# First loads of a two-layer attention and MLP kernel: bias rows and the second token tile on ScalarE's queue, key weights second on SyncE's queue, and a planner that counts some loads differently

## The chip, the cores and the metric

The kernel runs on one core of one Trainium2 chip. The metric is device time in microseconds (us). Times in a profile count from its first instruction. Engines are named as in the profile: PE is TensorE (matmuls), PEld its weight loads, DVE VectorE, ACT ScalarE, POOL GpSimd, SP SyncE, which issues nearly all DMAs. ACT can issue DMAs too; both feed the same DMA engines.

## What is computed

Two layers, each of a sliding-window attention and an MLP, both on a layer norm of the running x and both added to it. Tokens S = 2048, width D = 1024, hidden width F = 3584, 32 heads of 32; each token attends to itself and to 7 earlier tokens at a distance of 2, 4, ... 14.

```python
def _A_ref(x, wqkv, wo):
    H = 32; Dh = D // H
    W, dil = 8, 2
    qkv = (x @ wqkv).reshape(B, S, 3, H, Dh).transpose(2, 0, 3, 1, 4)
    ...
    logits = jnp.einsum("bhsd,bhswd->bhsw", q, kg) * scale
    attn = _softmax(jnp.where(mask, logits, -1e9), axis=-1)
    o = jnp.einsum("bhsw,bhswd->bhsd", attn, vg)
    return o.transpose(0, 2, 1, 3).reshape(B, S, D) @ wo

def _B_ref(x, w1, b1, w2, b2):
    r = jnp.maximum(x @ w1 + b1, 0)
    return (r * r) @ w2 + b2

x = x + _A_ref(_layernorm(x), A_wqkv, A_wo)
x = x + _B_ref(_layernorm(x), B_w1, B_b1, B_w2, B_b2)
# and the same two lines again with the same weights
```

## The kernel before, in words

**Units.** The work is cut into eight units, four blocks of 512 tokens in each of two layers. A unit's block is four token tiles of 128 rows. Even and odd tokens are held apart, so that a window is eight neighbours. A unit u goes through these stages, and TensorE interleaves the stages of neighbouring units:

- SA: load the four tiles, normalize, transpose into xnT (hidden width on the partitions).
- Projections: for keys (wk), queries (wq) and values (wv), eight chunks of 128 columns each (L481), and ACT copies each PSUM result to SBUF (L490: kT, qT, vT).
- S2: DVE multiplies shifted windows (product, L508), sums and softmax, and the values (L621 to L626). In unit 0 TensorE does the sums over a head's 32 columns (reduce, L520, into lg).
- SW: output projection (L671), add the residual (L674), normalize again.
- SF_up and SF_down: the MLP (L696, L721), with relu and square on ACT (L699, L701).

**What sets the order.** Each operation is entered into a planner (class _Plan) with an engine, an estimated duration, what it reads and writes, and for a DMA its bytes. The planner simulates the engines and issues operations by due time; each engine then runs its instructions in the order that came out. Operations marked main (nearly all of TensorE's) keep their written order. The simulation counts a DMA at DMA_RATE plus DMA_LAT, adds DMA_RAMP's second number of us once when the bytes moved pass its first number, and counts a further `lag` us between an operation's end and what depends on it. These numbers move instructions; they are not instructions. `issue_behind(a, b, ...)` makes the planner issue the named operations in that order.

**Memory.** All matmul results and PE transposes share six PSUM banks (tag "mm"). Weights share five SBUF buffers of 1 MB (tag "w"). The tiles of unit 1 and later, and the residual tiles, share two buffers (tag "xt").

**The opening** (first_projections, L752). TensorE first multiplies zeros (spin, L749: 11 matmuls of 512 columns, 6 of 128, and 2 more between the two transposes). Unit 0's tiles are normalized by DVE statistics (L370, L372), two small ACT steps (L373 lnv, L374 rstd), one DVE step (L388) and eight PE transposes (L403); DVE and ACT copy them out (L406, L407, L409). DVE's order there is written by hand: norm0 waits for tile 1's aggregate. Then come, in this order on TensorE: the key projections of the first 256 tokens in five chunks at once, step by step with the four pieces of the key weights as they land, then chunks 5 to 7; tile 2's transposes; the query projections of the first 256 tokens in the same way with the four query pieces, tile 3's transposes in their middle, then chunks 5 to 7; the second 256 tokens; the values.

**The loads of the opening.** SP issues (L418, L352) the tiles 0 and 1 of x, 256 KB each, four key pieces of 512 KB, tiles 2 and 3, four query pieces, then unit 1's first tile, the first half of the value weights, b1 (7 KB, L331), b2 (broadcast to 256 KB, L332), unit 1's next tile, and so on. ACT issues one small load (touch, L440) whose data nobody reads. SP waits, from the eighth load on, for an earlier landing before it issues the next, since eight completion semaphores are used in turn. b1 is transposed by one PE instruction (L334) and copied (L335) late in the opening.

**Unit 1's tiles** (and all later ones) are normalized on ACT: a sum (L380), the mean (L381), a sum of squares (L382), lnv (L384), rstd (L385), nmr (L386) and the normalized tile (L394); SP then issues a transposing DMA (L411).

Of the kernel before, what the change touches and what calls it, by code (L numbers as in the profile page):

```python
# [7 lines left out]
BF = mybir.dt.bfloat16  # L8
# [53 lines left out]
class _Plan:  # L62
# [5 lines left out]
    DMA_RATE = 390e3  # L68
    DMA_LAT = 2.2
    DMA_TR = 2.9  # L70
    DMA_RAMP = (600e3, 1.8)
    SMALL_FIRST = 1000.0

    @classmethod
# [90 lines left out]
    def schedule(self):  # L165
# [19 lines left out]
        while events:  # L185
# [19 lines left out]
            for e in self.ENGINES:  # L205
# [3 lines left out]
                while waiting[e]:  # L209
# [22 lines left out]
                    if op.dma:  # L232
                        if moved < self.DMA_RAMP[0] <= moved + abs(op.dma):
                            dma_free += self.DMA_RAMP[1]
                        moved += abs(op.dma)
# [24 lines left out]
class _Kernel:  # L260
# [61 lines left out]

    def load_biases(self):
        nc, add, KF, D = self.nc, self.plan.add, self.KF, self.D
        rows = self.plan.buf(self.small, [32, 128], BF, "b1rows")
        pt = self.plan.buf(self.ps, [128, 32], BF, "b1ps", "mm", 6)

        def zero():
            nc.vector.memset(rows.t[:], 0.0)
        add("DVE", 0.1, zero, w=[rows])  # L330
        add("SP", 0.5, lambda: nc.sync.dma_start(rows.t[:KF, :], self.b1.rearrange("(c p) -> c p", p=128)), w=[rows], dma=4e3)  # L331
        add("SP", 0.7, lambda: nc.sync.dma_start(self.b2b[:], self.b2.rearrange("(o d) -> o d", o=1).to_broadcast((128, D))), dma=262e3)  # L332
        self.plan.issue_behind(self.opened, self.plan.ops[-2], self.plan.ops[-1])
        add("PE", 0.1, lambda: nc.tensor.transpose(pt.t[:], rows.t[:], self.ident[0:32, 0:32]), r=[rows], w=[pt], main=True)  # L334
        add("DVE", 0.1, lambda: nc.vector.tensor_copy(self.b1T[:], pt.t[:, 0:KF]), r=[pt])  # L335


# [72 lines left out]
        else:  # L410
            add("SP", 1.25, lambda: nc.sync.dma_start_transpose(dst(), xn.t[:]), r=[xn], w=[lo, hi], dma=-690e3, lag=0.4)  # L411

    def load_x(self, layer, t, tag="xt", n=2):
        nc, D = self.nc, self.D
        b = self.plan.buf(self.sb, [128, D], F32, "xt", tag, n)
        if layer == 0:
            b.view = lambda: b.t[:].bitcast(BF)[:, 0:D]
            self.plan.add("SP", 0.5, lambda: nc.sync.dma_start(b.view(), self.par_tile(self.x_par, t)), w=[(b, 0), (b, 1)], dma=262e3)  # L418
        else:
            b.view = lambda: b.t[:]  # L420
            self.plan.add("SP", 0.55, lambda: nc.sync.dma_start(b.view(), self.xs[layer - 1][t * 128:(t + 1) * 128, :]),
                          w=[(b, 0), (b, 1)], dma=524e3, after=self.xs_parts[layer - 1, t])
        return b


    def SA(self, u):
        layer, b = divmod(u, self.NB)
        xnT = self.plan.buf(self.sb, [128, self.KD, BLK], BF, "xnT", "xnT", 2)
        self.state[u]["xnT_A"] = xnT
        first = u == 0  # L430
        if first:
            ops = self.plan.ops
            xts = [self.load_x(layer, tl, "xm", 4) for tl in range(4)]
            x0, x1, x2, x3 = ops[-4:]
            self.state[u]["wk"] = self.w_qkv(self.D, pieces=2)
            k = ops[-4:]
            self.state[u]["wq"] = self.w_qkv(0, pieces=2)
            q = ops[-4:]
            touch = self.plan.buf(self.small, [128, 32], BF, "touch")
            self.plan.add("ACT", 0.4, lambda: self.nc.scalar.dma_start(  # L440
                touch.t[:], self.wqkv.rearrange("(p e) n -> p e n", p=128)[:, 0, self.D:self.D + 32]), w=[touch], dma=8e3)
            self.plan.issue_behind(x0, x1, *k, x2, x3, *q)
            self.opened = q[-1]
        for tl in range(4):
            xt = xts[tl] if first else self.load_x(layer, b * 4 + tl)
            if u == 1:
                self.plan.issue_behind(self.opened, self.plan.ops[-1])
            norm = lambda tl=tl, xt=xt: self.layer_norm(xt, xnT, tl, dve_stats=first, pe_transpose=first)
            if first:
                yield norm  # L450
            else:
                norm()
# [406 lines left out]
```

## Time and profile before

| | |
|---|---|
| runs shown | 1236.03 us median of three, 1235.96 to 1236.37 |
| profiled execution | 1237.49 us, its span 1235.8 us |
| clock granted to TensorE | 1.000 |
| DMA | 255.16 MB, mean 206 GB/s |
| L696, L721, L481 on PE | 388.1, 388.3, 336.3 us busy |

The page gives the busy time and share of each engine and the chain of work that ended last: followed back from the last instruction, at each step to what released it, or to the instruction ahead of it on its engine. A row of the chain in order of time reads: start, length, engine and tile, line, number of instructions. "issue" is time in which an engine waited for nothing that the profile shows, and SPq is SP's queue. A row of a timeline reads: start, length from the first start to the last end, engine, line, operation, output from input with shapes and types, how many follow each other, and in square brackets the idle time of the engine ahead of it with what ended that. Ends of matmuls are modelled: they are pipelined, so their lengths overlap and their starts tell the pace. A row of a table by windows reads: the window, its length, busy time and number of instructions for PE, PEld, DVE, ACT and POOL, the granted clock, the mean share of the 16 DMA engines, and GB/s.

### The profile page before, as it was taken

Reading aid. Unit: us, or ns where it says so; the run is one execution under the profiler, and the core shown is the slowest. Engines: PE = TensorE matmul, PEld = TensorE weight load, DVE = VectorE, ACT = ScalarE, POOL = GpSimd, SP = SyncE. Lnnn points to the kernel's source line nnn. Section 1 sums busy time; section 2 is a strip of 40 time slices with the busy share of each in tenths; the row PEclk is TensorE's granted clock in tenths of the full one; section 3 lists DMA queues with packets and bytes.
Section 4 is the critical chain, followed back from the end, with each engine's and each line's share of the span. In section 5 each row is a group of like instructions: output and inputs, shape, how many; then the busy total and the mean of one; then the engine's idle time right before and its main releaser. Section 6 shows DMA issues by size and latency. Waiting matters only on the chain.

```text
span 1235.8 us, 15619 instructions
## 1 busy us (share of the span) xinstructions
PE 1228.7 (99%) x5914; PEld 638.4 (52%) x5914; DVE 825.3 (67%) x1233; ACT 565.4 (46%) x1031; POOL 180.2 (15%) x200
## 2 busy tenths in 40 slices
PE   8999999999999999999999999999999999999999
PEld 7765444554455544555445554455544564444444
DVE  5899885698806987079870899609885198972001
ACT  5627920488104881158801588016870146612720
POOL 1352000050500200005050020000505011000000
PEclk9999999999999999999999999999999999999999
DMA  6858767677567985588755996549965496567441
GB/s 231 254 189 223 220 215 229 187 231 222 170 213 186 264 249 167 191 222 277 218 187 171 247 282 214 175 152 283 261 206 174 165 255 199 165 191 235 151 136 55
DMA packets 258421, 255.16 MB, mean 206 GB/s; under 512 B 70602, under 2 KB 221354, under 8 KB 258346
## 3 DMA queue, kind: packets, MB, share of 16 engines
q1 hardware_dynamic: 258202, 254.16, 68.1%
q8 instruction: 46, 0.75, 0.3%
q14 instruction: 29, 0.24, 0.1%
q10 hardware_dynamic: 144, 0.01, 0.0%
HBM read 209.99 MB, written 12.58 MB: 180 GB/s over the span
## 4 chain that ended last, share of the span: by engine, by line
PE 98%; DMA 1%; ACT 0%; SPq 0%; issue 0%; DVE 0%
PE ph L696 31%; PE py L721 31%; PE pq L481 26%; PE py L671 9%; DMA xt<-in_A_x_dram 1%; DMA wt<-in_A_wqkv_dram 1%; PE lg L520 0%; ACT xn L382 0%; ACT xn L380 0%; SPq L352 0%; SPq L418 0%; DVE xo L731 0%; ACT qT L490 0%; ACT nmean L381 0%; PE b1ps L334 0%
## 5 line engine op out<-in xcount | busy, mean ns | idle before, releaser
L721 PE MATMUL py<-wt,r2t 128*128 128x512 bf16 (+1 forms) x1820 | 388.3, 376 | 0.0
L696 PE MATMUL ph<-xnT,wt 128*128 128x512 bf16 x1792 | 388.1, 379 | 0.1
L481 PE MATMUL pq<-xnT,wt 128*128 128x512 bf16 (+2 forms) x1674 | 336.3, 362 | 1.5 <-ACT qT L490 1.4
L721 PEld LDWEIGHTS <-r2t 128*128 128x128 bf16 x1820 | 178.1, 98 | 209.0
L481 PEld LDWEIGHTS <-wt 128*128 128x128 bf16 x1674 | 229.9, 144 | 106.3 <-issue 2.8
L696 PEld LDWEIGHTS <-wt 128*128 128x128 bf16 x1792 | 175.2, 98 | 211.5 <-issue 0.6
L490 ACT CAST kT<-pq 128x512 bf16<-128x512 f32 (+1 forms) x72 | 38.6, 543 | 353.5 <-PE pq L481 353.5
L699 ACT ACTIVATE r<-ph,b1T 128x512 bf16<-128x512 f32 x224 | 152.4, 682 | 70.8 <-PE ph L696 70.7
L508 DVE TENSOR_TENSOR P<-qT,kT 128x2048 bf16<-128x2048 bf16 x128 | 154.0, 1235 | 10.6 <-ACT qT L490 5.0
L621 DVE TENSOR_TENSOR pr<-pb,vT 128x2048 bf16<-128x2048 bf16 x128 | 153.4, 1234 | 7.3 <-DMA pb<-p 7.2
L701 ACT ACTIVATE r2t<-r 128x512 bf16<-128x512 bf16 x224 | 139.1, 628 | 5.3
L731 DVE TENSOR_TENSOR xo<-py,xm 128x512 bf16<-128x512 f32 (+1 forms) x33 | 22.3, 675 | 159.2 <-PE py L721 155.8
L624 DVE TENSOR_TENSOR pr<-pr 128x1024 bf16<-128x1024 bf16 (+1 forms) x256 | 126.8, 552 | 0.0
L525 DVE TENSOR_TENSOR P<-P 128x2048 bf16<-128x2048 bf16 x98 | 118.9, 1221 | 1.2
L671 PE MATMUL py<-wt,oT 128*128 128x512 bf16 x512 | 111.8, 379 | 0.0
L674 DVE TENSOR_TENSOR xm<-py,xt 128x512 f32<-128x512 f32 x64 | 43.1, 684 | 94.9 <-PE py L671 94.0
L497 POOL COPY vhalo<-vT 128x7 bf16<-128x7 bf16 x64 | 59.3, 939 | 228.8 <-ACT vT L490 228.7
L497 POOL COPY khalo<-kT 128x7 bf16<-128x7 bf16 x64 | 20.0, 315 | 483.2 <-ACT kT L490 483.0
L471 POOL COPY vT<-vhalo 128x7 bf16<-128x7 bf16 x32 | 68.2, 2183 | 123.6 <-DVE pr L621 123.5
L671 PEld LDWEIGHTS <-oT 128*128 128x128 bf16 x512 | 50.1, 98 | 60.1
L735 DVE TENSOR_TENSOR xm<-py,xm 128x512 f32<-128x512 f32 x32 | 22.0, 690 | 84.1 <-PE py L721 84.1
L373 ACT ACTIVATE lnv<-mv,eps 128x1 f32<-128x1 f32 x36 | 10.5, 291 | 92.6 <-DVE mv L372 92.5
(61 smaller groups left out, 545.7 us busy)
## 6 DMA issues: line engine op xcount, KB each, us to landing
wt<-in_B_w_dram SPq DMA_DIRECT2D x56, 1024.0 KB, 7.0
wt<-in_B_w_dram SPq DMA_DIRECT2D x64, 896.0 KB, 4.8
wt<-in_A_wqkv_dram SPq DMA_DIRECT2D x44, 1024.0 KB, 6.2
wt<-in_A_wo_dram SPq DMA_DIRECT2D x16, 1024.0 KB, 5.8
xt<-xs SPq DMA_DIRECT2D x32, 512.0 KB, 3.6
xt<-in_A_x_dram SPq DMA_DIRECT2D x32, 256.0 KB, 3.3
pb<-p SPq DMA_DIRECT2D x64, 128.0 KB, 5.1
xs<-xm SPq DMA_DIRECT2D x32, 256.0 KB, 3.4
```

Source lines behind the costliest of these rows:

```text
L471: add("POOL", 0.2, lambda: nc.gpsimd.tensor_copy(dst.t[:, 0:off], prev.t[:, c0, :]), r=[(prev, c0)], w=[(dst, 0)])
L481: nc.tensor.matmul(pq.t[:, a - t0:b - t0], w[:, kd % 4, c0:D:8], xnT.t[:, kd, a:b], start=first and kd == k0, stop=last and kd == k1 - 1, ...
L497: add("POOL", 0.2, lambda: nc.gpsimd.tensor_copy(halo.t[:, c0, :], dst.t[:, BLK:BLK + HALO]), r=[(dst, 2)], w=[(halo, c0)])
L508: st["dve"].append(add("DVE", 1.14, lambda: nc.vector.tensor_tensor(P.t[:], q.t[:, hb * HB:(hb + 1) * HB].rearrange("q (g t) -> q g t", g= ...
L525: self.state[u]["dve"].append(self.plan.add("DVE", 1.14, lambda: self.nc.vector.tensor_tensor(a.t[:], a.t[:], b.t[:], ALU.add), r=[b], w=[a]))
L621: dve.append(add("DVE", 1.14, lambda v=v, pr=pr: nc.vector.tensor_tensor(pr.t[:], pb.t[:], _win_ap(v.t, HALO + hb * HB, HB, groups=G), ALU ...
L624: dve.append(add("DVE", d, lambda pr=pr, k=k: nc.vector.tensor_tensor(pr.t[:, :, 0:k, :], pr.t[:, :, 0:k, :], pr.t[:, :, k:2 * k, :], ALU. ...
L671: nc.tensor.matmul(py.t[:], st["o", c].t[:, tl * 128:(tl + 1) * 128], st["wo"][db].t[:, c, :], start=(c == 0), stop=(c == self.NCH - 1))
L696: nc.tensor.matmul(ph.t[:], wt.t[:, kd, cc * 128:(cc + 1) * 128], xnT.t[:, kd, :], start=(kd == 0), stop=(kd == self.KD - 1))
L699: add("ACT", 0.58, lambda ph=ph, r=r, f=f: nc.scalar.activation(out=r.t[:], in_=ph.t[:], func=ACTF.Relu, bias=self.b1T[:, f:f + 1], scale= ...
L701: add("ACT", 0.54, lambda r=r, r2t=r2t: nc.scalar.activation(out=r2t.t[:], in_=r.t[:], func=ACTF.Square), r=[r], w=[r2t])
L721: nc.tensor.matmul(py.t[:], r2[kf].t[:, tl * 128:(tl + 1) * 128], wt.t[:, kf - k0, c0:c1], start=(kf == 0), stop=(kf == KF - 1))
```

## The change

- Unit 0's second tile (tl == 1) is loaded from ACT's queue, behind the rows of b1, which are now loaded there first. The small load "touch" is gone.
- SP's order begins with tile 0 and the four key pieces, then tiles 2 and 3 and the query pieces. b1 is no more among SP's loads.
- The tile of b1's rows has 28 rows rather than 32, so the DVE memset of it is gone, and the PE transpose has 28 columns.
- The planner counts a ramp of 0.4 us rather than 1.8 at 600 KB, and unit 1's tiles 2.0 us later (lag).

```diff
-    DMA_RAMP = (600e3, 1.8)
+    DMA_RAMP = (600e3, 0.4)
...
     def load_biases(self):
-        rows = self.plan.buf(self.small, [32, 128], BF, "b1rows")
+        rows = self.b1rows
         pt = self.plan.buf(self.ps, [128, 32], BF, "b1ps", "mm", 6)
-
-        def zero():
-            nc.vector.memset(rows.t[:], 0.0)
-        add("DVE", 0.1, zero, w=[rows])
-        add("SP", 0.5, lambda: nc.sync.dma_start(rows.t[:KF, :], self.b1.rearrange("(c p) -> c p", p=128)), w=[rows], dma=4e3)
         add("SP", 0.7, lambda: nc.sync.dma_start(self.b2b[:], self.b2.rearrange("(o d) -> o d", o=1).to_broadcast((128, D))), dma=262e3)
-        self.plan.issue_behind(self.opened, self.plan.ops[-2], self.plan.ops[-1])
-        add("PE", 0.1, lambda: nc.tensor.transpose(pt.t[:], rows.t[:], self.ident[0:32, 0:32]), r=[rows], w=[pt], main=True)
+        self.plan.issue_behind(self.opened, self.plan.ops[-1])
+        add("PE", 0.1, lambda: nc.tensor.transpose(pt.t[:, 0:KF], rows.t[:], self.ident[0:KF, 0:KF]), r=[rows], w=[pt], main=True)
...
-    def load_x(self, layer, t, tag="xt", n=2):
+    def load_x(self, layer, t, tag="xt", n=2, eng="SP", lag=0.0):
...
-            self.plan.add("SP", 0.5, lambda: nc.sync.dma_start(b.view(), self.par_tile(self.x_par, t)), w=[(b, 0), (b, 1)], dma=262e3)
+            self.plan.add(eng, 0.47, lambda: (nc.sync if eng == "SP" else nc.scalar).dma_start(b.view(), self.par_tile(self.x_par, t)),
+                          w=[(b, 0), (b, 1)], dma=262e3, lag=lag)
...
-            xts = [self.load_x(layer, tl, "xm", 4) for tl in range(4)]
+            self.b1rows = rows = self.plan.buf(self.small, [self.KF, 128], BF, "b1rows")
+            b1 = self.plan.add("ACT", 0.47, lambda: self.nc.scalar.dma_start(rows.t[:], self.b1.rearrange("(c p) -> c p", p=128)), w=[rows], dma=7e3)
+            xts = [self.load_x(layer, tl, "xm", 4, "ACT" if tl == 1 else "SP") for tl in range(4)]
             x0, x1, x2, x3 = ops[-4:]
+            self.plan.issue_behind(b1, x1)
...
-            touch = self.plan.buf(self.small, [128, 32], BF, "touch")
-            self.plan.add("ACT", 0.4, lambda: self.nc.scalar.dma_start(
-                touch.t[:], self.wqkv.rearrange("(p e) n -> p e n", p=128)[:, 0, self.D:self.D + 32]), w=[touch], dma=8e3)
-            self.plan.issue_behind(x0, x1, *k, x2, x3, *q)
-            self.opened = q[-1]
+            self.plan.issue_behind(x0, *k, x2, x3, *ops[-4:])
+            self.opened = ops[-1]
...
-            xt = xts[tl] if first else self.load_x(layer, b * 4 + tl)
+            xt = xts[tl] if first else self.load_x(layer, b * 4 + tl, lag=2.0 if u == 1 else 0.0)
```

What the planner makes of it, by the built programs (each row is an order on one engine; "xn0 of unit 1" is its first tile):

```
ACT before: ... kT x6, lnv, rstd, kT, lnv, rstd, kT, L380 xn0 of unit 1, L381, L382, qT x6, L380, ...
ACT after:  ... kT x2, lnv, kT, rstd, kT x2, lnv, kT, rstd, kT x2, L380 xn0 of unit 1, qT x5, L381, L382, qT x2, L380, ...
PE:   one group of 8 matmuls (L481) stands behind the first lg reduction instead of ahead of it, and is made up for ahead of the third
DVE:  the second softmax's reciprocal (L600) stands ahead of the first product of the values instead of behind four chunks
SP:   unit 0's two first residual tiles are issued in turn with unit 1's third and fourth transposing DMA instead of behind both
```

Behind unit 1's stages the orders are the same again. Lines of the kernel below the change shift by five.

More of the change, by code (lines that the diff above doesn't have):

```diff
@@ L437, in SA @@
             self.state[u]["wq"] = self.w_qkv(0, pieces=2)
-            q = ops[-4:]
-            touch = self.plan.buf(self.small, [128, 32], BF, "touch")
-            self.plan.add("ACT", 0.4, lambda: self.nc.scalar.dma_start(
-                touch.t[:], self.wqkv.rearrange("(p e) n -> p e n", p=128)[:, 0, self.D:self.D + 32]), w=[touch], dma=8e3)
-            self.plan.issue_behind(x0, x1, *k, x2, x3, *q)
-            self.opened = q[-1]
+            self.plan.issue_behind(x0, *k, x2, x3, *ops[-4:])
+            self.opened = ops[-1]
         for tl in range(4):
-            xt = xts[tl] if first else self.load_x(layer, b * 4 + tl)
+            xt = xts[tl] if first else self.load_x(layer, b * 4 + tl, lag=2.0 if u == 1 else 0.0)
             if u == 1:
```

## The prediction

> **What bounds the kernel now.** I read the page first, then the chain of work that ended last, then the timelines of TensorE and ScalarE around the only long hole that the chain shows, then the DMA rates of the opening.
>
> ```profile
> span 1235.8 us, 15619 instructions
> PE 1228.7 (99%) x5914; PEld 638.4 (52%) x5914; DVE 825.3 (67%) x1233; ACT 565.4 (46%) x1031; POOL 180.2 (15%) x200
> PE 98%; DMA 1%; ACT 0%; SPq 0%; issue 0%; DVE 0%
> ```
>
> TensorE is busy for 99% of the span and is 98% of the chain. So a change of loads can only win what TensorE loses in the opening, and can lose anywhere that it makes TensorE wait. The chain in order of time shows where the opening ends:
>
> ```profile
> 2.72 8.03 DMA wt<-in_A_wqkv_dram
> 10.75 0.02 issue
> 10.77 10.18 DMA xt<-in_A_x_dram
> 20.95 0.02 issue
> 20.97 1.16 ACT xn L380 x2
> 22.13 0.02 issue
> 22.16 0.21 ACT nmean L381
> 22.37 0.02 issue
> 22.39 1.24 ACT xn L382 x2
> 23.63 0.27 ACT qT L490
> 23.90 0.04 issue
> 23.94 6.27 PE pq L481 x56
> ```
>
> From 23.94 us to the end the chain is TensorE alone, but for 0.13 us at 113.5 and the last store. Before that it runs through something that TensorE does not need yet: the first token tile of unit 1 (L418, issued at 10.77, landed at 20.95) and its statistics on ScalarE (L380 to L382). The two timelines say why this stops TensorE:
>
> ```profile
> 19.16 3.35 PE L481 MATMUL pq<-xnT,wt 128*128 128x256 bf16 x28
> 23.94 0.27 PE L481 MATMUL pq<-xnT,wt 128*128 128x256 bf16 x1 [1.44 <-ACT qT L490]
> ```
>
> ```profile
> 20.97 1.06 ACT L380 ACTIVATE xn<-xt 128x1024 bf16<-128x1024 bf16 x1 [4.47 <-DMA xt<-in_A_x_dram]
> ...
> 23.54 1.72 ACT L490 CAST qT<-pq 128x256 bf16<-128x256 f32 x6
> ```
>
> ScalarE runs in order. L380 stands ahead of the evictions of the query projections and waits 4.47 us for its tile; all six "mm" banks are full, and TensorE waits for the first eviction. The idle time is 1.44 us by the modelled end of a matmul (22.51); matmuls of this width start 0.11 apart and last 0.27, so some 1.6 us are lost (22.34 to 23.94). Call the restart R; it is 23.94. What follows R is 1211.9 us of dense work.
>
> **The change, part by part.** R is the later of two times: when TensorE gets there by itself, and when ScalarE has freed a bank.
>
> *ScalarE's order* (lag of 2.0 and the ramp figure; both are the planner's counts and cost no instruction). In the built order L380 of unit 1's first tile is now followed by five qT evictions, and L381 and L382 come after these; the load's place on SP's queue stays. The first eviction then starts 1.09 after the tile lands (20.95 to 22.04: the 1.06 of L380 and its 0.19 read, overlapped) instead of 23.54. From that eviction's start to R it takes 0.40 as now (23.54 to 23.94). With the tile landing as now, R would be 22.44: 1.50 saved. The removed 1.5 us of L381 and L382 run after the five evictions, under 5.4 us of matmuls.
>
> *The load stream.* SP's second load leaves its queue, so the four key pieces are issued one slot earlier: 0.47 (1.27 for 1.74). ScalarE's queue issues the bias rows and the second tile, 0.40 each as the touch load took; ScalarE idles 3.49 before its first instruction at 5.58, which hides it. The touch and the late bias load (0.95 on SP at 12.86) go; nobody waited for either, and SP then waits for earlier landings anyway. What more the stream gains hangs on its slow start:
>
> ```profile
> 2.00:4.00 2.00, 2.00 (x6) 0.76 (x5) 0.44 (x1) 0.08 (x1) 0.40 (x2) 1.00 0.83 269
> 4.00:6.00 2.00, 2.00 (x13) 0.92 (x10) 2.00 (x5) 0.39 (x2) 0.00 (x0) 1.00 0.64 200
> 6.00:8.00 2.00, 1.32 (x21) 1.01 (x18) 1.67 (x5) 0.68 (x4) 0.00 (x0) 1.00 0.95 359
> 8.00:12.00 4.00, 3.95 (x43) 3.43 (x40) 0.42 (x1) 1.10 (x2) 0.00 (x0) 1.00 1.05 400
> 12.00:16.00 4.00, 3.96 (x36) 3.70 (x34) 3.17 (x7) 2.97 (x11) 0.00 (x0) 1.00 1.06 391
> ```
>
> The last column is GB/s. Against 395 the first three stretches are short by 2x126, 2x195 and 2x36, that is 714 KB or 1.8 us. Nothing here proves what a second queue or the missing touch does to that, so the stream's gain lies between 0 and 0.47 + 1.8 = 2.3 us (below 0 only through the second tile, a rival). I take 1.0: the slot and about a third of the shortfall, nearer to the end that needs nothing unseen. Behind 8 us the stream runs at its full rate, so a gain at the start is carried to every landing after it, unit 1's tile too: 19.95, and the bank is free at 21.44.
>
> [...]
>
> *TensorE by itself.* Its first projection starts at 8.18, when piece one lands (1.74 + 6.4 = 8.1), but also when the transposes of tiles 0 and 1 are over (7.54 + 0.62 = 8.16). Those hang on DVE's chain from the tiles: statistics at 3.56, and the third of them needs tile 1 by about 4.8 (it lands at 1.27 + 3.3 = 4.6). So earlier key weights alone start nothing earlier. From 8.18 to 22.34 TensorE then loses, by distance of starts, 0.20 and 0.20 for key pieces three and four (the weight loader shows 0.27 and 0.28), 0.13 for tile 2 at 16.06 and 0.07 for the last query piece: 0.6. A stream earlier by 1.0 removes these, so TensorE arrives at 21.7. Were tiles 0 and 1 normalized 0.1 earlier, without the touch's 8 KB beside them, 21.6. The bank is free at 21.44, so R = 21.7: **2.2 us less**. A stream gaining more than 1.0 adds nothing, since TensorE is the limit from there.
>
> *Statistics of tiles 2 and 3 on ScalarE.* Their lnv now stands behind two key evictions instead of six. Behind it wait six evictions, and TensorE for their banks. Tile 2's mv came 2.0 after it landed (14.8; landed about 12.8), so 13.8 now; the third eviction is done 0.3 later, at 14.2, and its bank is wanted by tile 2's transposes at about 15.4. Cover 1.2; without the stream's gain about 0.2. Nothing.
>
> *Order behind R.* One group of eight matmuls moves behind the first lg reduction, which now comes 6 x 0.895 = 5.4 after R. DVE's four products take 4 x 1.17 = 4.7 from R, so 0.6 of cover is left of 1.5. DVE's second reciprocal (0.55) moves into its 0.88 wait for pb: slightly better. POOL's one swap and the missing memset (0.11) are nothing. Unit 1's third and fourth tile are normalized later: adding the reordered ScalarE rows behind R, the last L394 ends near R+25.6, where it was 45.18 = R+21.2. Their DMA transposes now stand behind two residual loads. In before SP's issue of them was held to 53.26 by a full DMA queue, and unit 1's projections start at about 58; I estimate 1 to 2 us of cover left. Nothing, with a rival.
>
> *Sum.* Of the profiled execution (1237.49, span 1235.8) this leaves a span of 1233.6 and 1235.3. The median of the runs shown is 1236.03, 1.46 below that execution; the same 2.2 off it gives **1233.8**.
>
> **The rivals.**
>
> 1. *The stream hardly moves.* For it: the 16 engines are full from 8 us on, and no row shows the shortfall to be the queue's. At a gain of 0.47, key piece four lands at 11.64 and tile 2 is ready 0.3 late, TensorE arrives at 22.0 and the bank is free at 21.97: 1.9 saved, 1234.1. At 0 it is 1.5 saved, 1234.5. [...] Chance 0.22.
>
> 2. *Tiles 0 and 1 come earlier too.* The touch is gone and tile 1 has a queue of its own. DVE's chain can move until its transposes meet the end of the warm-up matmuls (6.14, where 6.81 stands now): 0.6. With the stream 1.5 earlier R is 21.0: 2.9 saved, 1233.1. Against it: tile 1 now shares the engines with the key weights. Chance 0.18.
>
> 3. *Slower: the second tile starves.* On ScalarE's queue it runs beside key weights that were behind it. DVE's third statistic holds up tile 0's aggregate as well, so every us of landing after 4.8 delays the first projection. R = 21.66 + d reaches 23.94 at d = 2.3, so it decides from a landing at 7.1. Behind all four pieces (2.1 MB at 395 GB/s, 5.3 us) it lands at 9.9: d = 5.1, R = 26.8, 1238.9. Against it: the touch, issued from that queue at 0.83, landed 2.9 later, beside tiles 0 and 1. Chance 0.06.
>
> 4. *Unit 1's late transposes.* If the queue delays them beyond their cover, TensorE stops at unit 1's key projections, near 56 us; 1 to 3 us, so 1234.8 to 1236.8. Chance 0.10.
>
> **How the numbers follow.** The forecast has 0.44, with a range of its own from 1233.4 to 1234.2. The range of 1233.0 to 1235.2 leaves out rival 3, most of rival 4 and the low half of rival 2, under 2 in 10. 0.2% is 2.5 us, about what a measurement of this kernel can tell from no change, so "faster" begins below 1233.56: rival 2 and some 4 in 10 of the forecast, 0.36. "Slower" is rival 3 and a trace of rival 4, 0.07. The rest, 0.57, is within.
>
> **What would show it.** Right: L380 waits less than 4.47 and five qT follow it; TensorE's longest idle time behind 8 us is under 0.3; R is 21.4 to 22.0; the key pieces land about 1.0 earlier than 8.1, 9.4, 10.7 and 12.1; 4 to 6 us runs well above 200 GB/s; no idle time near 56 us. Wrong: tile 1 lands after 4.8 and the first projection starts later than 8.2; a wait for lg's products near R+5.4; or a saving that differs from the shift of R, which would put the cause behind the opening.

## The result, and the profile after

The changed kernel takes 1237.88 us (median of 22 runs, 1236.58 to 1239.92), the kernel before 1236.24 (22 runs beside them, 1235.75 to 1238.01). The ratio is 1.0012, interval [1.0006, 1.0017]: slower by 0.12%, within the 0.2% that the prediction called no change, but on the other side of the forecast and outside its range.

The times of the changed kernel fall into two groups: 11 of 22 at 1236.6 to 1237.6 with a mean granted clock of 1.000, and 11 at 1238.2 to 1239.9 with 0.997 to 0.999. The kernel before shows 1.000 in all its runs beside the experiments below. The profile taken of the changed kernel (1237.11) belongs to the first group, so it doesn't show what the second group has on top. Its page (the rows of the span, of the engines and of the chain):

```profile
span 1235.3 us, 15618 instructions
...
PE 1228.4 (99%) x5914; PEld 638.6 (52%) x5914; DVE 825.7 (67%) x1232; ACT 565.3 (46%) x1031; POOL 181.9 (15%) x200
...
PE 99%; DMA 1%; DVE 0%; ACT 0%; issue 0%; ACTq 0%
```

TensorE's share of the chain rises from 98% to 99%: the long stall at the restart is gone. The lines of the changed file stand five lower (L481 is L476 now, L490 L485, L380 L375, L403 L398). The chain in order of time, from its start:

```profile
1.50 4.65 DMA xt<-in_A_x_dram
6.16 0.02 issue
6.18 0.69 DVE stats L365
...
8.25 0.62 PE pt L398 x8
...
9.61 7.21 PE pq L476 x74
16.82 0.45 PE pt L398 x8
17.26 2.19 PE pq L476 x20
19.45 0.45 PE pt L398 x8
19.90 8.31 PE pq L476 x76
28.21 0.98 PE lg L515 x16
```

The chain now begins with the second token tile: issued on ACT's queue at 1.50, landed at 6.16. In before it landed at 4.56, 3.29 behind its issue at 1.27. From the first projection on there is TensorE alone: 76 matmuls run through the place where before stopped after 28. VectorE's timeline shows how the tile reaches TensorE (two rows), and TensorE's own what it costs there:

```profile
3.65 1.28 DVE L365 BATCH_NORM_STATS2 stats<-xt 128x6 f32<-128x512 bf16 x2 [1.73 <-DMA xt<-in_A_x_dram]
6.18 0.69 DVE L365 BATCH_NORM_STATS2 stats<-xt 128x6 f32<-128x512 bf16 x1 [1.25 <-DMA xt<-in_A_x_dram]
```

```profile
8.25 0.62 PE L398 MATMUL pt<-ident,xn 128*128 128x128 bf16 x8 [1.39 <-DVE xn L383]
```

The third statistic, tile 1's first, waits 1.25 us; in before the three ran back to back. The transposes start at 8.25 instead of 6.81, the first projection at 9.44 (timeline) instead of 8.18. ScalarE at the restart, and the rates of the opening (last column GB/s, PEclk before the DMA share):

```profile
19.29 1.06 ACT L375 ACTIVATE xn<-xt 128x1024 bf16<-128x1024 bf16 x1 [2.06 <-DMA xt<-in_A_x_dram]
20.25 0.19 ACT L375 ACTIVATION_READ_ACCUMULATOR xn<-xt 128x1 f32 x1
21.26 1.48 ACT L485 CAST qT<-pq 128x256 bf16<-128x256 f32 x5 [0.82 <-PE pq L476]
```

```profile
2.00:4.00 2.00, 2.00 (x6) 0.73 (x5) 0.35 (x1) 0.08 (x1) 0.40 (x2) 1.00 0.84 268
4.00:6.00 2.00, 2.00 (x7) 0.61 (x5) 0.94 (x2) 0.00 (x0) 0.00 (x0) 1.00 1.02 331
6.00:8.00 2.00, 0.86 (x8) 0.44 (x6) 1.78 (x5) 0.68 (x3) 0.00 (x0) 1.00 1.03 395
```

L375 waits 2.06 instead of 4.47, five evictions follow it, and they wait for TensorE, not it for them. The stretch from 4 to 6 us moves 331 GB/s instead of 200. The key pieces land at 5.95, 7.85, 9.19 and 10.55 instead of 8.13, 9.40, 10.75 and 12.11. So the stream and the order did what they should, and the second tile took much of it back.

The restart R, the start of the 29th matmul behind tile 3's transposes, lies inside the run of 76 now, at 22.80 instead of 23.94. That is 1.14 earlier, yet the span is only 0.5 shorter. The prediction named such a difference as a sign of a cause behind the opening, and there are two. Ahead of L691 at 112.7 (L696 in before) TensorE loses 0.2 more than in before. And the end of the program got longer; the chain's last row in before, then in the changed kernel:

```profile
1232.80 0.42 DVE xo L731
```

```profile
1231.87 0.42 DVE xo L726
```

From the end of this row to the end of the span it takes 2.5 us in before (1235.8) and 3.0 in the changed kernel (1235.3). In the profiles of before, e12, e7 and e3 it is 2.5, in that of e13 2.6, and in the other eleven, all with changed loads, 2.9 to 3.0. Why is open; 0.4 of the loss against before lies there, and it isn't the second tile's, since e1 and e5 have it too.

### The profile page after: what moved, and what is told of

Its sections match the earlier page's. It is cut to its first block, busy times and chain, and to the rows that moved or that the text cites. A ratio compares the mean times of both kernels' runs of the same rounds, so it can differ in the third digit from the quotient of the medians.

```text
span 1235.3 us, 15618 instructions
## 1 busy us (share of the span) xinstructions
PE 1228.4 (99%) x5914; PEld 638.6 (52%) x5914; DVE 825.7 (67%) x1232; ACT 565.3 (46%) x1031; POOL 181.9 (15%) x200
## 4 chain that ended last, share of the span: by engine, by line
PE 99%; DMA 1%; DVE 0%; ACT 0%; issue 0%; ACTq 0%
PE ph L691 31%; PE py L716 31%; PE pq L476 27%; PE py L666 9%; DMA xt<-in_A_x_dram 0%; PE lg L515 0%; DMA xnT<-xn 0%; PE pt L398 0%; DVE stats L365 0%; ACT L288 0%; DVE xo L726 0%; DVE xn L383 0%; DVE mv L367 0%; ACT vT L485 0%; PE b1ps L329 0%
## 5 line engine op out<-in xcount | busy, mean ns | idle before, releaser
L691 PE MATMUL ph<-xnT,wt 128*128 128x512 bf16 x1792 | 388.1, 379 | 0.3 <-DMA xnT<-xn 0.3
L476 PE MATMUL pq<-xnT,wt 128*128 128x512 bf16 (+2 forms) x1674 | 335.6, 362 | 0.0
L691 PEld LDWEIGHTS <-wt 128*128 128x128 bf16 x1792 | 175.3, 98 | 211.7 <-issue 0.7
L476 PEld LDWEIGHTS <-wt 128*128 128x128 bf16 x1674 | 229.9, 144 | 103.9 <-issue 1.7
L485 ACT CAST kT<-pq 128x512 bf16<-128x512 f32 (+1 forms) x72 | 38.7, 543 | 354.8 <-PE pq L476 354.8
L696 ACT ACTIVATE r2t<-r 128x512 bf16<-128x512 bf16 x224 | 139.1, 628 | 5.4
```

What stands on the lines that cost most here:

```text
L476: nc.tensor.matmul(pq.t[:, a - t0:b - t0], w[:, kd % 4, c0:D:8], xnT.t[:, kd, a:b], start=first and kd == k0, stop=last and kd == k1 - 1, ...
L691: nc.tensor.matmul(ph.t[:], wt.t[:, kd, cc * 128:(cc + 1) * 128], xnT.t[:, kd, :], start=(kd == 0), stop=(kd == self.KD - 1))
L696: add("ACT", 0.54, lambda r=r, r2t=r2t: nc.scalar.activation(out=r2t.t[:], in_=r.t[:], func=ACTF.Square), r=[r], w=[r2t])
```

## The experiments

Each median is given with that of the kernel before in the same batch. "Landing" is that of unit 0's second tile unless said otherwise.

Two theories at first. **Late tile and clock**: the tile's place behind the first key piece costs about 1 us in each execution, and in about half of them the longer idle time of TensorE makes its clock fall, for about 2 us more. **Rival**: something behind the opening (the planner's order, or the fetch of other code) splits and slows the runs.

**e0: the changed kernel again.** No edit.

> The changed kernel unedited, beside the edited ones. In its profile tile 1 (the second token tile of unit 0, on ScalarE's queue) landed at 6.16 us and the first projection started at 9.44 to 9.61; the granted clock averaged 1.000 in about half of its executions (1236.6 to 1237.6 us) and 0.997 to 0.999 in the others (1238.2 to 1239.9). Theory (late tile, then clock): the same two groups again, landing 6.0 to 6.4, and a profile with a mean clock under 1.000 shows the clock rising later or falling once in the first 20 us, with matmuls at half pace there. Rival (something behind the opening varies, such as a load): the slow group has its loss behind 20 us, at full clock.

1238.41 (11 runs), before 1236.31, ratio 1.0015 [1.0007, 1.0024]; two groups again. Its profile (1239.16) fell in the upper one: landing 7.29, and the trace's clock records give full clock from 6.95 for 3.41 us, half clock from 10.36 for 3.41, and full clock from 13.78 on. Ahead of its first clock record the PEclk column shows 1.00 all the same, though the warm-up matmuls of 512 columns start 0.43 apart there and 0.22 apart at full clock (e11). Rows by those three stretches:

```profile
6.95:10.36 3.41, 1.19 (x18) 0.84 (x17) 2.83 (x7) 0.99 (x4) 0.00 (x0) 1.00 1.05 404
10.36:13.78 3.42, 3.42 (x32) 3.22 (x30) 2.73 (x7) 1.17 (x2) 0.00 (x0) 0.50 1.05 388
13.78:17.19 3.41, 3.41 (x33) 3.41 (x32) 0.57 (x3) 1.26 (x6) 0.00 (x0) 1.00 1.05 386
```

In the first stretch TensorE was busy for 1.19 of 3.41 us; the next ran at half clock. R is 25.37 here and 22.52 in the profile of e1 (next), and from R on both take 1211.9 to 1212.0. So the loss against e1 lies ahead of R, as the first theory says.

**e1: the second tile back on SP, second; all else as changed.**

```diff
-            xts = [self.load_x(layer, tl, "xm", 4, "ACT" if tl == 1 else "SP") for tl in range(4)]
+            xts = [self.load_x(layer, tl, "xm", 4, "SP") for tl in range(4)]
-            self.plan.issue_behind(b1, x1)
-            self.plan.issue_behind(x0, *k, x2, x3, *ops[-4:])
+            self.plan.issue_behind(x0, x1, *k, x2, x3, *ops[-4:])
```

> The changed kernel with tile 1 back on SP's queue, second, ahead of the key weights; bias rows still on ScalarE's queue, no touch load, planner as changed. Theory: tile 1 lands by 4.7, the first projection starts by 8.3, the restart that was 23.94 in before needs no wait for a bank, at 21.7 to 22.2, and the time is 1233.8 to 1234.4, in one group with a mean clock of 1.000. If the touch load was what slowed the stream at 4 to 6 us (200 GB/s in before), that stretch now shows over 300; if it was the place of the key weights, it stays near 200. Rival (the reordered engines cost the time): 1236 and more, although the tile lands early.

1235.99, before 1236.31, ratio 0.9997 [0.9988, 1.0006]; all runs at clock 1.000 within 0.7 us. Landing 4.42, first projection 8.31. So the loss against before is gone once the tile is back in its old place. The time is not the 1233.8 to 1234.4 that was expected, though, and it stands at the edge of the rival's 1236: TensorE does not wait at the restart, but R is 22.52, later than the 21.7 to 22.2 expected, and the end of the program is the longer one. The edit also takes the stream's gain away: 239 GB/s from 4 to 6 us, fourth key piece at 12.32. There is no touch load in this kernel, but b1's 7 KB are issued in its place, at 0.83; that they don't hold the stream back is seen in e8, which has them too.

**e2: the changed kernel with TensorE kept busy for longer.**

```diff
         self.spin(6, 128)
+        self.spin(20, 128, 0.0)    # 20 more matmuls of 128 zero columns, counted as 0 by the planner
```

> The changed kernel with 20 more zero matmuls of 128 columns ahead of the first transposes, at no cost to the planner, so that all other orders stay. At full clock they fill 1.1 us of the 1.39 us in which TensorE is idle ahead of the first transposes. Theory (the idle time lets the clock fall or rise late in some executions): all executions at a mean clock of 0.999 or more and 1236.5 to 1237.3, the upper group gone; median 1236.9. Rival (the clock has nothing to do with that idle time): half of them stay above 1238. A third way: where the clock rises late, 20 more matmuls at half pace last 2.2 us and delay the transposes by up to 0.8.

1237.54, before 1236.31, ratio 1.0008 [0.9999, 1.0017]. The upper group is gone: no run above 1237.94, ten of eleven at 1.000. What stays is a lower group (1236.6 to 1236.7) and one of 1237.2 to 1237.9, nearly all at full clock. The median is 0.6 above the expected 1236.9, so more than the clock separates the executions; the tile still lands late.

**e3: the planner's two figures alone, on the kernel before.**

```diff
-    DMA_RAMP = (600e3, 1.8)
+    DMA_RAMP = (600e3, 0.4)
...
+            xt = xts[tl] if first else self.load_x(layer, b * 4 + tl, lag=2.0 if u == 1 else 0.0)
```

> The kernel before with the planner's two figures alone (ramp 0.4, unit 1's tiles 2.0 later): loads and queues as before. Theory: TensorE's wait of 1.6 us ahead of 23.94 shrinks to about 0.1 since five evictions stand ahead of L381 and L382, restart at 22.4 to 22.6, 1.4 to 1.5 us less than before: 1234.6 to 1234.9. Rival (the new order makes another wait): the restart is 22.5 and the time is 1235.5 or more.

1235.95, before 1236.31, ratio 0.9998 [0.999, 1.0007], all runs between 1235.8 and 1236.7. The predicted 1.5 us of this edit isn't there. In this profile unit 1's tile landed at 19.19, and ScalarE shows

```profile
19.21 1.06 ACT L380 ACTIVATE xn<-xt 128x1024 bf16<-128x1024 bf16 x1 [2.47 <-DMA xt<-in_A_x_dram]
20.18 0.19 ACT L380 ACTIVATION_READ_ACCUMULATOR xn<-xt 128x1 f32 x1
20.36 1.48 ACT L490 CAST qT<-pq 128x256 bf16<-128x256 f32 x5
```

With a landing at 19.2 the order hardly matters, so this profile doesn't test it. With L381 and L382 ahead of them the evictions would have begun at 21.78 (19.21 plus the 2.57 that L380 to L382 took in before, 20.97 to 23.54) and TensorE gone on 0.40 later, at 22.2: 0.3 behind the 21.9 at which it gets there by itself here. By the spans inside the runs the gain is 0.7 (medians 1233.9 and 1234.6): the time outside the span is some 0.3 longer in e3's runs than in those of before.

**e4: the loads alone** (the changed kernel with the planner's figures of before).

```diff
-    DMA_RAMP = (600e3, 0.4)
+    DMA_RAMP = (600e3, 1.8)
...
-            xt = xts[tl] if first else self.load_x(layer, b * 4 + tl, lag=2.0 if u == 1 else 0.0)
+            xt = xts[tl] if first else self.load_x(layer, b * 4 + tl, lag=0.0)
```

> The changed kernel with the planner's two figures as in the kernel before: only the loads differ, and five query evictions stand ahead of unit 1's statistics or behind them as that planner has it. Theory (the order is worth nothing in a typical execution, the tile's late landing is the whole loss): 1237.3 to 1238.6, two groups as the changed kernel, ratio 1.0008 to 1.0020. Rival (the order saves 1.5, as predicted, and the loads lose 3): 1239 to 1240.5, ratio 1.0023 or more, and a wait of TensorE at the restart of over 1 us.

1239.01, before 1236.54, ratio 1.0021 [1.0012, 1.0030]; ten of eleven runs at 0.997 to 0.999. This is worse than the first theory expected, and by the time it is the rival's 1239 to 1240.5 (its ratio of 1.0023 is just missed), but it isn't the rival's mechanism: its profile has no wait at the restart (with these loads the planner itself puts five query evictions ahead of L375). It has a landing at 7.32, transposes at 9.41 and half clock for two stretches of 3.41 us. Whether it lands late more often than the changed kernel, or by chance did so here, is open.

Next question: is it ACT's queue that is slow, or the place in time behind the first key piece (issued at 1.25, the tile at 1.50)?

**e5: the tile first on ACT's queue, the bias rows behind it.**

```diff
-            self.plan.issue_behind(b1, x1)
+            self.plan.issue_behind(x1, b1)
```

> The changed kernel with one pair of issues swapped: ScalarE issues the second token tile first (at about 0.83) and the bias rows behind it. Theory (place): the tile landed at 6.16 because it was issued at 1.50, behind the first key piece (1.26), and was served behind it; issued ahead of it, it lands at 4.3 to 5.0, the first projection starts at 8.0 to 8.4, the key pieces keep what they gained (landings about 6.2, 7.9, 9.3, 10.6), nothing waits at the restart, no execution loses clock: 1235.2 to 1235.9, one group of times, ratio 0.9992 to 0.9998. Rival (queue): a 128x1024 load on ScalarE's queue is slow in the opening wherever it stands; it then lands at about 5.5 (0.67 earlier than 6.16, like its issue) or later, the first projection starts at 8.8 or later, and the time stays at 1236.6 or above, some executions at a clock below 1.000.

1236.10, before 1236.54, ratio 0.9996 [0.9988, 1.0005], clock 1.000 in all runs, spread 0.55 us. Time from issue to landing, e5 and then the changed kernel:

```profile
xt<-in_A_x_dram SPq DMA_DIRECT2D x1, 256.0 KB, 3.6
xt<-in_A_x_dram ACTq DMA_DIRECT2D x1, 256.0 KB, 3.7
```

```profile
wt<-in_A_wqkv_dram SPq DMA_DIRECT2D x1, 512.0 KB, 4.7
xt<-in_A_x_dram SPq DMA_DIRECT2D x1, 256.0 KB, 2.8
xt<-in_A_x_dram ACTq DMA_DIRECT2D x1, 256.0 KB, 4.7
```

Issued at 0.83, ahead of the key piece, it lands at 4.54: the queue as such isn't slow, the place is what counts. But tile 0, now in flight beside it, lands at 4.37 instead of 3.6 (3.6 behind its issue instead of 2.8), and tile 0 starts VectorE's chain. Transposes start at 7.65 and the first projection at 8.84, later than the 8.0 to 8.4 expected, and the time is above the expected 1235.2 to 1235.9. From there TensorE is dense; R is 22.19.

**e8: the tile on SP's queue, behind the first key piece.**

```diff
-            self.plan.issue_behind(x0, *k, x2, x3, *ops[-4:])
+            self.plan.issue_behind(x0, k[0], x1, *k[1:], x2, x3, *ops[-4:])
```

> The changed kernel with the second token tile on SP's queue, but behind the first key piece, so its place in the stream is kept and its queue is changed. Theory (place): it lands at 5.8 to 6.8, the first projection starts at 9.2 to 10.0, and the times are those of the changed kernel: 1236.6 to 1239.9 in two groups, median 1237 to 1238.5. Rival (queue): on SP it lands before 5.2, the first projection starts at 8.5 or earlier, and the median is 1235.7 to 1236.3 at a clock of 1.000.

1237.46, before 1236.54, ratio 1.0006 [0.9997, 1.0014]; 5 of 11 runs at 0.999. Landing 6.35, first projection 9.57 (timeline): the same as in the changed kernel's first profile, on ACT's queue. Its times end at 1238.42 and its clocks at 0.999, where the changed kernel's go to 1240.28 and 0.997, so the queue may add something in some executions; one profile can't tell. And the key pieces land at 5.03, 7.90, 9.26 and 10.61 with no load but b1's 7 KB on ACT's queue. With the tile second on SP the fourth piece landed at 11.72 to 12.32 (five profiles: before, e1, e3, e7, e12), with the tile on ACT's queue at 10.37 to 11.12 (seven). So the gain comes with a key piece second on SP's queue and needs no load on a second queue, nor does a small load there prevent it. Why a tile in that place slows the stream stays open.

**e7: before, with shorter warm-up.**

```diff
-        self.spin(11)
+        self.spin(7, BLK, 11 / 7 * BLK * 8.3e-4)    # 7 matmuls, the planner's cost of 11
```

> The kernel before with 7 instead of 11 warm-up matmuls of 512 columns, and the planner's cost for them unchanged: the same loads, the same order on every engine, but TensorE idle for about 0.9 to 1.7 us longer ahead of its first transposes (1.5 to 2.4 in all). Theory (clock): in a share of the executions the clock falls to half for some 3.4 us behind that idle time; these show a mean clock of 0.997 to 0.999 and take 1.5 to 2.5 us longer, so two groups, and a median anywhere from 1236 to 1238. Rival (the late tile itself, or the loads, splits the times): the loads are as before, so one group at 1.000 and 1235.7 to 1236.5, ratio 0.9995 to 1.0005.

1236.20, before 1236.54, ratio 0.9996 [0.9987, 1.0006], all at 1.000: the clock did not fall. The idle time came to 1.29 in its profile, and the full clock was granted only at 6.25; in the 3.41 us behind that TensorE was busy for 2.83. So the edit did not bring the idle time of 1.5 to 2.4 that was meant, and 1.29 is below the 1.39 at which the changed kernel's first profile kept its clock: e7 doesn't decide whether the length of the idle time matters. e8 and e0 do:

```profile
8.38 0.62 PE L398 MATMUL pt<-ident,xn 128*128 128x128 bf16 x8 [2.39 <-DVE xn L383]
```

```profile
9.38 0.62 PE L398 MATMUL pt<-ident,xn 128*128 128x128 bf16 x8 [2.22 <-DVE xn L383]
```

In e8 (first row) TensorE idled for longer than in e0, and e8 kept its full clock. So it isn't the length alone; the next runs ask for the share of a stretch. e7 also shows before's stall again (see e12).

**e10, e11, e12: one more profiled execution each** of e2, of the changed kernel and of before, with landing, clock and time of the same execution.

> The changed kernel with 20 more short warm-up matmuls again, one look. Theory (the second tile lands at about 6.2 in some executions and at about 7.3 in others): a span of 1234.7 to 1235.0 goes with a landing near 6.2, one of 1235.4 to 1236.2 with a landing of 6.8 to 7.4, and TensorE is dense from the first projection to the end of the restart in both, at full clock. Rival (the landing is always near 6.2 and something later splits the times): a span of over 1235.4 with a landing below 6.4.

Landing 6.38, full clock, span 1235.0: a case of the low group. The higher one wasn't caught, so that its 1.0 us is a landing near 7.3 remains an inference.

> The changed kernel again, one look. Theory (the clock falls where TensorE is busy for less than some 0.4 of the 3.41 us behind the moment at which the clock is granted): with a landing near 6.2 the share is over 0.4, the clock stays full and the span is 1234.5 to 1235.5; with a landing near 7.3 the share may be below, and then the clock is half for 3.41 or 6.83 us and the span 1236.5 to 1238.5. Rival (the clock falls by chance or by the length of the idle time alone): a fall at a share over 0.45, or none at a share below 0.33.

1239.40, landing 7.15, transposes at 9.24 (TensorE idle for 2.97). Full clock was granted at 5.12; the three stretches behind that:

```profile
5.12:8.53 3.41, 1.15 (x10) 0.62 (x8) 1.36 (x3) 0.49 (x2) 0.00 (x0) 1.00 1.02 364
8.53:11.94 3.41, 2.70 (x26) 2.70 (x27) 2.15 (x7) 1.19 (x5) 0.00 (x0) 0.50 1.05 395
11.94:15.35 3.41, 3.41 (x40) 3.41 (x39) 2.53 (x6) 0.51 (x2) 0.00 (x0) 1.00 1.05 388
```

The same rows of the changed kernel's first profile, of e8 and of e4, each from the moment at which full clock was granted:

```profile
6.33:9.74 3.41, 2.02 (x30) 1.64 (x29) 2.88 (x8) 1.37 (x5) 0.00 (x0) 1.00 1.05 403
9.74:13.15 3.41, 3.41 (x40) 3.41 (x39) 2.23 (x5) 0.80 (x2) 0.00 (x0) 1.00 1.05 389
```

```profile
4.55:7.96 3.41, 1.44 (x11) 0.71 (x9) 2.11 (x6) 0.52 (x3) 0.00 (x0) 1.00 0.91 302
7.96:11.37 3.41, 2.99 (x43) 2.83 (x44) 1.79 (x5) 1.65 (x4) 0.00 (x0) 1.00 1.06 399
```

```profile
4.99:8.40 3.41, 1.22 (x10) 0.61 (x8) 1.06 (x3) 0.22 (x1) 0.00 (x0) 1.00 0.99 349
8.40:11.81 3.41, 2.40 (x23) 2.40 (x24) 2.15 (x6) 1.36 (x5) 0.00 (x0) 0.50 1.06 403
11.81:15.23 3.42, 3.42 (x27) 3.03 (x25) 2.82 (x7) 0.58 (x1) 0.00 (x0) 0.50 1.04 385
```

Divide the first busy time of each row by 3.41: at 0.34 (e11), 0.35 (e0) and 0.36 (e4) the next stretch ran at half clock, at 0.42 (e8), 0.59 (the changed kernel) and 0.83 (e7) it did not. Of the stretches at half clock, the one at 0.70 (e4) was followed by another at half, those at 0.79 (e11) and 1.00 (e0, e4) by full clock. The other ten profiled executions have a mean clock of 1.000; in before's the stretch with the stall at the restart (21.57 to 24.99) is at 0.58, and full clock follows it. So until the program ends the clock fell behind the three stretches at 0.34 to 0.36 and behind no other, while the length of the idle time does not order them (2.39 in e8 without a fall, 2.22 in e0 with one). What sets the clock is not shown by that; the expectation's "some 0.4" was the author's estimate, between 0.36 (e4) and 0.42 (e8). The moment at which full clock was granted differs from execution to execution (6.33, 6.95 and 5.12 in three profiles of the changed kernel), and so does the landing (6.16, 7.29 and 7.15), so the busy share of the stretch differs too (0.59, 0.35 and 0.34): one kernel gives two groups.

What makes a landing 7.2 rather than 6.2: in e11, DMA packets between 6 and 7 us by queue (q10 is ACT's)

```profile
q1 hardware_dynamic: 189, 0.37, 99.8%
q10 hardware_dynamic: 5, 0.01, 2.9%
```

Five packets of ACT's queue are left over there; the changed kernel's first profile has none of q10 behind 6 us. In e11 the tile waits for its last few packets, beside a stream that fills the engines.

> The kernel before, one look. Theory (the wait at the restart hangs on when unit 1's first tile lands, which differs by over 1 us from execution to execution): with a landing of 20.5 or later TensorE waits over 1 us at the restart and the span is 1235 or more; with a landing of 19.2 to 19.7 it waits under 0.4 and the span is 1234.6 or less. Rival (the wait is always there, and the spread of the times is elsewhere): a wait of over 1 us with a span below 1234.6.

1238.01, near the top of the 15 runs of before beside it (1235.75 to 1238.14): unit 1's tile landed at 21.02, and TensorE shows at the restart

```profile
24.01 6.28 PE L481 MATMUL pq<-xnT,wt 128*128 128x256 bf16 x56 [1.43 <-ACT qT L490]
```

All three profiled executions with the old order and loads (before, e7, e12) have this wait of 1.43 or 1.44, landings of 20.95, 20.82 and 21.02, and spans of 1235.8, 1235.3 and 1236.3. In e7 the span is second longest of eleven (1233.9 to 1235.5), in e12 near the top of 1234.0 to 1236.4. So the profiled execution stood at the long end. An execution at 1234.4 can't have had the whole wait, if the rest is equal; none such was profiled. The landings show where the lateness arises: the second and third query piece land 2.6 to 2.9 apart in these three profiles (16.17 and 18.91 in before) and 1.3 apart in e3 (15.79 and 17.10), which has the same loads. What holds the third piece up in one execution and not in another is open, as is whether that is what parts before's short executions from its long ones.

**e9, e13, e14: can both gains be had?** The tile second on SP, and the first key piece on ACT's queue behind the bias rows; e13 and e14 move only the planner's lag.

```diff
-                    nc.sync.dma_start(b.t[:].rearrange("p (a b) n -> p a (b n)", a=4)[:, j * n:(j + 1) * n, :],
+                    (nc.scalar if act and k0 == 0 else nc.sync).dma_start(b.t[:].rearrange("p (a b) n -> p a (b n)", a=4)[:, j * n:(j + 1) * n, :],
...
-            self.plan.issue_behind(b1, x1)
+            self.plan.issue_behind(b1, k[0])
-            self.plan.issue_behind(x0, *k, x2, x3, *ops[-4:])
+            self.plan.issue_behind(x0, x1, *k[1:], x2, x3, *ops[-4:])
...
-            xt = xts[tl] if first else self.load_x(layer, b * 4 + tl, lag=2.0 if u == 1 else 0.0)
+            xt = xts[tl] if first else self.load_x(layer, b * 4 + tl, lag=3.0 if u == 1 else 0.0)    # e13; 6.0 in e14
```

> The changed kernel with two transfers exchanged: the second token tile is SP's second load again, and the first key piece goes on ScalarE's queue, behind the bias rows. Theory (a transfer of one queue is served about in the order of issue, and the first two tiles bound TensorE's start): the second tile lands at 4.4 to 5.0, the first projection starts at 7.9 to 8.3, the key pieces land 0.4 to 1.5 earlier than in the kernel before, nothing waits behind them: spans of 1233.2 to 1233.9, 1235.0 to 1235.8, one group at a clock of 1.000, ratio 0.9988 to 0.9996, the fastest of all. Rival (ScalarE's queue is served late whatever it carries): the first key piece lands behind the second, at 9 or later, the first projection waits for it, and the time is 1236.2 or more.

1236.71, before 1236.28, ratio 0.9999 [0.9990, 1.0008]: not the fastest. The loads went as expected (landing 4.51, key pieces 6.45 to 10.59, first projection 8.23). But the planner, given these loads, put L375 to L377 ahead of the query evictions again, and TensorE waits twice:

```profile
14.16 1.91 PE L477 MATMUL pq<-xnT,wt 128*128 128x256 bf16 x16 [0.31 <-ACT kT L486]
...
22.59 5.40 PE L477 MATMUL pq<-xnT,wt 128*128 128x256 bf16 x48 [0.37 <-ACT qT L486]
```

> The exchange of the second tile and the first key piece again, with the planner's lag for unit 1's loads at 3.0 in place of 2.0, so that ScalarE's order at the restart is that of the changed kernel (L375, five query evictions, then L376 and L377). Theory (the order at the restart costs only in the executions in which unit 1's tile lands late, and the exchange itself gains a little at the start): no wait of over 0.2 at the restart, the upper half of the times of the run with lag 2.0 (spans of 1235.0 to 1235.6) is gone, spans of 1233.3 to 1234.4, median 1235.2 to 1236.0, ratio 0.9990 to 0.9998. Rival (the upper half comes from something else than the restart): two groups again, median 1236.3 to 1237.0.

1236.25, before 1236.37, ratio 0.9997 [0.9989, 1.0006]. The wait at the restart is gone, the upper runs are not (spans 1233.7 to 1235.6 in one spread), and the expected 1235.2 to 1236.0 is missed. The key piece on ACT's queue landed at 7.83 this time, 6.3 behind its issue, and the first of the waits grew:

```profile
15.00 1.91 PE L477 MATMUL pq<-xnT,wt 128*128 128x256 bf16 x16 [1.19 <-ACT kT L486]
```

> The same with a lag of 6.0: all six query evictions that the first banks need stand ahead of unit 1's L375, so that the landing of unit 1's tile can't stop TensorE at the restart. Theory: as with 3.0, 1235.2 to 1236.0, within 0.3 of it, and the least spread. Rival (unit 1's statistics are then late, and its last transposed tiles hold up its projections near 56 us): a wait of TensorE near 56 us of 0.5 to 2 us, and 1236.0 to 1237.5.

1236.80, before 1236.37, ratio 1.0003 [0.9994, 1.0012]. The time is the rival's, its mechanism isn't: there is no wait of TensorE at the restart and none near 56 us, but the key piece landed at 9.15, and TensorE waited 0.72 for it and 0.71 for a kT eviction. Three profiles of one set of loads have landings of 6.45, 7.83 and 9.15 for this piece. So a 512 KB transfer on ACT's queue beside SP's stream landed 4.9 to 7.6 behind its issue, as the 256 KB tile in that place landed 4.7 to 5.8 behind its own.

No version is measurably faster than before. The lowest ratios are e5's 0.9996, e7's 0.9996, e1's and e13's 0.9997 and e3's 0.9998, and all their intervals hold 1.

## Why the prediction was wrong

- **What bounds the kernel.** TensorE in the opening, and R: right as a mechanism for the execution shown. Wrong as a base: the stall of 1.6 us that carried the forecast belongs to the long executions. Taking it off the median was the first failed step. (The interval of the ratio is 0.11% wide here: the runs tell smaller changes apart than the 0.2% that the prediction allowed for.)
- **ScalarE's order, 1.5.** Mis-sized for the median: e3 shows 0.36 (1235.95 for 1236.31, 0.7 by the spans), an interval that holds 0. What goes with it is the end of before's upper tail, up to 1237.87 in that batch: e3 ends at 1236.69, and e1 and e5, with the same order, at 1236.48 and 1236.50. That the order does this by taking away the wait is not shown, since e3's tile landed early.
- **The load stream, 1.0 of at most 2.3.** Too low: the key pieces came 1.5 to 2.2 earlier. Unit 1's tile landed at 19.26 where 19.95 was forecast. The place of the shortfall, 4 to 6 us, was right. A second queue is not what brought it: in e8, with SP alone and a key piece second, the last piece is as early (10.61), 1.50 ahead of before's 12.11. So the order on one queue moved it by 1.5 us, where the forecast counted 1.0, with 0.47 of it for the slot.
- **TensorE by itself, with tile 1 landing as now.** This is the step that failed and turned the sign: "tile 1 by about 4.8 (it lands at 1.27 + 3.3 = 4.6)" was carried over to another queue and place. It landed at 6.16 to 7.32 in six profiles of tiles on ACT's queue behind the key piece. This is rival 3, held at 0.06, at a landing below its point of decision: its own formula R = 21.66 + d gives 23.02 at a landing of 6.16, against the 22.80 measured. That its 1238.9 lies inside the upper group is luck: it was worked out for a landing at 9.9, at full clock. Its argument against itself, the touch that landed within 2.9, was 8 KB issued at 0.83, ahead of the key pieces; the tile was issued behind one.
- **What no step had: the clock.** The fall of the clock in half of the executions. From the profile at 1237.11 to e11 the tile is 0.99 later, the transposes 0.99, but the start of the 76 matmuls 1.97 (19.90 to 21.87): 0.98 is the clock's share. In e0 it is 1.44 (transposes 1.13 later, matmuls 2.57). In e4, with two slow stretches, transposes are 1.16 later and those matmuls 3.56 (23.46), so 2.40.
- **Sum as it came out.** For the lower group e5 is the closest comparison, since it has the same stream and differs only in when the tile is issued: 0.60 at the first projection (9.44 for 8.84) and 0.61 at R (22.80 for 22.19); the lower group's times of 1236.6 to 1237.6 stand 0.5 to 1.5 above e5's 1236.10. Against e1 the first projection is 1.13 later (9.44 for 8.31), but R only 0.28 (22.80 for 22.52), as the earlier key pieces make up the rest; e1's profile is of its slowest run. In the upper group come some 1 us for a landing near 7.2 and 1 to 2.4 for the clock. Against before there are also 0.4 at the end of the program, which the prediction's sum had at nothing.
- **Statistics of tiles 2 and 3, order behind R, unit 1's late transposes.** Costed at nothing, and the trace agrees: TensorE is dense from the first projection until it idles 0.3 ahead of L691 at 112.7 (0.13 in before, but 0.62 in e12, the same kernel), and has no idle time near 56 us. Rival 4 did not occur. (That a full queue held SP to 53.26 in before was the author's reading: the two issues of L411 took 4.00 and 2.78 us there, with the DMA share at 1.10.) Rival 1 and 2 fell with the stream's gain and the tile's landing.

## What to carry to other kernels

A load moved to another queue has a new place in time as well (here it was issued at 1.50 for 1.27 and landed at 6.16 for 4.56): before taking its old landing over, ask which large transfer is now issued before it, and which engine's chain starts with it. A stall read from one execution may belong to that execution: set its time against the spread of the others before subtracting it from the median. And TensorE's idle time ahead of the real work had a second price here, a granted clock of 0.50 for 3.41 or 6.83 us, worth 0.98 to 2.40 us in three profiles. So keep it busy until the work comes (e2: no run above 1237.94), or bring the work early (e1, e5: all runs at 1.000).

## What the runs showed of the hardware beyond that

- The granted clock was 0.50 for 3.41 us (e11, e0) or 6.83 us (e4) behind 3.41 us in which TensorE was busy for 0.34, 0.35 and 0.36 of the time; behind 0.42 (e8), 0.59 (the changed kernel) and 0.83 (e7) it was not.
- Two 256 KB tiles issued on two queues at 0.81 and 0.83 landed at 4.37 and 4.54 (e5), where one after the other on SP they landed at 3.4 to 3.6 and 4.4 to 5.1 (eight profiles): the later one hardly gained, and the first lost some 0.8 to 0.9.
- From 4 to 6 us the DMA engines moved 178 to 243 GB/s where all the early tiles and key pieces were on SP's queue (before, e1, e3, e7, e8, e12), and 297 to 365 where one of them was on ACT's (nine profiles; the tenth, e14, shows 239). The last key piece was not the earlier for it, since e8's came at 10.61.
